# Causal pairs of the third layer alternate with unmasked pairs, under a new table of planner settings

## The chip, the cores and the metric

One core of a Trainium2 chip. The metric is the device time of one execution in microseconds (us), lower is better. The engines are TensorE (PE, matrix products into PSUM), ScalarE (ACT), VectorE (DVE), GpSimd (POOL) and SyncE (SP, which issues the DMAs).

## The reference

Four transformer layers over 2048 tokens of width 512, 32 heads of 16, all in bfloat16. Layers 0 and 2 (kind A; the third layer is layer 2) split the tokens into 4 segments of 512; within a segment attention is causal, and a running memory matrix of the earlier segments is mixed in through a gate. Layers 1 and 3 (kind B) are unmasked attention over all 2048 keys. Cut to what matters:

```python
for s in range(4):                                   # layers 0 and 2
    qs, ks, vs = q[:, :, s], k[:, :, s], v[:, :, s]
    p = softmax(einsum('bhqd,bhkd->bhqk', qs, ks) * scale + mask)
    a_dot = einsum('bhqk,bhkd->bhqd', p, vs)
    a_mem = (phi(qs) @ M) / (phi(qs) @ z + 1e-6)
    outs.append(g * a_mem + (1 - g) * a_dot)
    M, z = M + phi(ks).T @ vs, z + phi(ks).sum()
...
p = softmax(einsum('bhqd,bhkd->bhqk', q, k) * Dh ** -0.5)   # layers 1 and 3
x = x + attention(layernorm(x)) @ wo                        # every layer
```

## The kernel before

The cost is in the exponentials of the scores. The kernel works in tiles of 128 keys by 512 queries for one head. Eight heads share a chunk `c` of 128 rows; a *group* is the four even or four odd heads (`e`) of a chunk for one segment of queries, and the two groups of a chunk make a *pair*. An unmasked group against all keys has 64 tiles; a causal group of 12 has the tiles `k2`, `k13` and `k0` (256, 512 and 512 columns), which leave out the masked blocks.

A *unit* is two or three tiles in adjacent PSUM banks: PE writes the scores (L445), one ACT instruction takes the exponential of up to 1536 columns into `pT` (L1514), POOL clears the masked triangle of causal tiles (L1529), and two or three units later PE multiplies by the values into one accumulator bank. Two sets of three banks alternate between units. Beside this, DVE computes the exponential of some tiles (`dx`): a first step (`dx_first`, L1121) writes scaled scores as integers whose bits are a bfloat16, and two or three shifts (`dx_shift`, L1184) give its further terms; each term has a value product of its own on PE. Such tiles need free DVE time, buffers (`dxw`, and the space of tensors no longer in use), and a free bank. Only unmasked tiles are taken (`dx_find`).

The program has no loop on the chip: a planner in Python writes all instructions out, with its own estimates of when each engine is free. `attention` goes from unit to unit; `select` picks the next pair from two lists, `seqA` (causal) and `seqB` (unmasked), as soon as its inputs are planned; `compose` decides which tiles go to DVE; `background` puts in projections, layer norms, memory updates and output products where credits (`CR_A`, `CR_W`, `CR_LOW`) allow; `keep_busy` adds a product of `zero` with `wB` (a *filler*) where PE would otherwise be thinly used (`FILL`, `FILLS`). `TAKEN` limits how many tiles of a group go to DVE, `REST` and `DQ` when one may be taken, `LOW` and `AHEAD` tell when work is short. The class holds a value of each setting, and the table `PIECES` changes them at times of the planner's own clock for ACT, about every 40 us.

The lines that the change touches in effect are those of `select` (L1392 on):

```python
        if not self.ALT and len(self.sel) > 2 and self.seqA and self.seqA[0][0].L and all(g.kind == "B" and not g.pos for g in tail) and ...:
            ...                                   # an unmasked pair not yet begun is handed back
            self.seqB.insert(0, tail)
        while len(self.qm_free) > 1 and (...):
            pair = None
            spread = self.ALT and self.seqA and self.seqA[0][0].L and self.seqA[0][0].qseg < self.ALTS and (0 < self.run_b < self.ALT or self.run_a >= self.ALTA[self.seqA[0][0].qseg])
            for seq in (self.seqB, self.seqA) if spread else (self.seqA, self.seqB):
                if seq and self.met(self.group_needs(seq[0][0])):
                    pair = seq.pop(0)
                    self.run_a, self.run_b = (self.run_a + 1, 0) if pair[0].kind == "A" else (0, self.run_b + 1)
                    break
```

With `ALT = 0` the causal list always comes first: all pairs of a segment of the third layer whose inputs are there run in a row, ahead of unmasked pairs of the second layer. When both kinds are chosen, the masked queries of a pair (`qm`, L1424) are made on DVE, else on POOL.

Of the kernel before, what the change touches and what calls it, by code (L numbers as in the profile page):

```python
# [257 lines left out]
class Builder:  # L258
    NPU, NDX, FIT, MARGIN, PART, FILL_DVE, EARLY, FILL = 4, 5, 2, 450, 1, 300, 700, 0.5
    FILLS, DVE_FIN, DX_FIN, EVAC_ACT, DX_BANK, DX_LATE, BG_BANK, DVE_LATE = 2, 600, 2000, 0, 500, 3000, 200, 1000  # L260
    DVE_LATE_LOW, CR_A, CR_B, CR_W, CR_LOW, CARRY, CARRY_W, REST = 9000000000.0, 1300, 1500, 1400, 1900, 0, 0, 11
    NEAR, SLACK, ALT3, ALT5, GAP, AHEAD, PE_B, PE_A = 10, 300, 2, 4, 2, 300, 4, 5
# [5 lines left out]
    DX_RES, CHAINS, ALT, ALTS, ALTA = 0, 4, 0, 3, (1, 1, 1, 1)  # L268
# [12 lines left out]
              (420.0, {'DMA_LATE': 300, 'DMA_STEPS': 3, 'DQ': 2500, 'DX_RES': 2, 'DX_T': 330, 'FILLS': 1, 'HOR': 100, 'MARGIN': 700, 'NEAR': 6, 'NEAR_E': 0, 'NEAR_N': 200}),  # L281
              (460.0, {'ALTA': (1, 9, 9, 9), 'DMA_LATE': 300, 'DMA_STEPS': 3, 'DQ': 2500, 'DX_RES': 2, 'DX_T': 330, 'FILLS': 1, 'HOR': 100, 'MARGIN': 700, 'NEAR': 10, 'NEAR_E': 0, 'NEAR_N': 200, 'TAKEN': 1.5}),
              (500.0, {'ALTA': (1, 1, 9, 9), 'CR_W': 1250, 'DMA_LATE': 600, 'DMA_STEPS': 2, 'DQ': 2200, 'DQN': 300, 'DX_RES': 0, 'DX_T': 430, 'FILLS': 2, 'HOR': 400, 'MARGIN': 450, 'NEAR_E': 60, 'NEAR_N': 130, 'TAKEN': 2.7}),
              (540.0, {'ALTA': (1, 1, 1, 1), 'CR_W': 1400, 'DQ': 2500, 'DQN': 600, 'PE_A': 4}),
              (580.0, {'DQ': 2200, 'FILLS': 1, 'FILL_DVE': 450, 'PART': 3, 'PE_A': 5}),
              (620.0, {'FILLS': 1, 'FILL_DVE': 450, 'NEAR_S': 30, 'PART': 3, 'SLACK': 150}),
              (660.0, {'FILLS': 2, 'FILL_DVE': 300, 'NEAR_S': 60, 'PART': 1, 'SLACK': 0}),
              (700.0, {'MARGIN': 700, 'SLACK': 0, 'TAKEN': 2.4}),
              (740.0, {'DQ': 2500, 'DX_LATE': 1500, 'MARGIN': 700, 'SLACK': 0, 'TAKEN': 2.4}),
              (780.0, {'DQ': 2200, 'DX_LATE': 3000, 'MARGIN': 450, 'PVHOLE': 250, 'PVLATE': 600, 'SLACK': 300, 'TAKEN': 2.7}),  # L290
              (820.0, {'BG_BANK': 0, 'PVHOLE': 100, 'PVLATE': 900, 'TAKEN': 3}),
              (860.0, {'AHEAD': 200, 'BG_BANK': 200, 'TAKEN': 2.7}),
# [1593 lines left out]
```

## Time and profile before

| | us |
|---|---|
| median of 3 runs | 1779.52 |
| lowest, highest | 1776.07, 1780.4 |
| the profiled execution | 1777.42 |
| its span | 1775.7 |
| ACT busy | 1733.2 (98%) |
| PE busy | 1586.7 (89%) |
| DVE busy | 1520.6 (86%) |
| POOL busy | 287.4 (16%) |

The span is the stretch from the first to the last instruction. Each line of a profile names the engine, the line of the kernel, the operation, the tiles written and read (out<-in), their shapes, and the count; "idle before" is the time the engine sat idle just before, with what ended it.

### The profile page before, as it was taken

What the parts mean: (1) busy time and instruction counts of PE and PEld (TensorE: products, weight loads), DVE (VectorE), ACT (ScalarE), POOL (GpSimd) and SP (SyncE); (2) the same over time, 40 slices, a digit from 0 to 9 for tenths busy, and PEclk for the clock granted to TensorE, in tenths of its full rate; (3) what the DMA queues carried; (4) which work ended last, traced back from release to release, by engine and by line L of the source; (5) the groups of instructions that cost most, each with busy time, mean ns of one, the idle gap of its engine ahead of it and who ended that gap; (6) DMA issues with size and microseconds to landing.
All of it is one profiled execution on the core that took longest, in us unless ns stands there. A gap on an engine that the chain in (4) does not pass through costs nothing.

```text
span 1775.7 us, 42674 instructions
## 1 busy us (share of the span) xinstructions
PE 1586.7 (89%) x17429; PEld 564.7 (32%) x17429; DVE 1520.6 (86%) x3016; ACT 1733.2 (98%) x1680; POOL 287.4 (16%) x656
## 2 busy tenths in 40 slices
PE   8889899999998999999999989999888888888887
PEld 4445454452223222323222332332222222222222
DVE  6677867499985999798999789767999999999998
ACT  7999999999999999999999999999999999999998
POOL 4622415110005000203000330241100000000000
PEclk9999999999999999999999999999999999999999
DMA  6121111000101000000000010010000000000000
GB/s 173 22 47 32 29 17 26 14 12 4 16 7 16 1 13 13 8 13 19 1 13 13 16 23 13 16 22 13 2 13 1 1 1 13 1 1 7 7 1 13
DMA packets 86180, 30.01 MB, mean 17 GB/s; under 512 B 78816, under 2 KB 85472, under 8 KB 85984
## 3 DMA queue, kind: packets, MB, share of 16 engines
q1 hardware_dynamic: 85984, 27.29, 7.5%
q8 instruction: 136, 2.23, 0.5%
q14 instruction: 60, 0.49, 0.1%
HBM read 6.30 MB, written 2.10 MB: 5 GB/s over the span
## 4 chain that ended last, share of the span: by engine, by line
ACT 50%; PE 22%; issue 16%; DVE 9%; POOL 2%; DMA 1%; SPq 0%; ACTq 0%; DVEq 0%; POOLq 0%
ACT pT L1514 49%; PE ps L445 22%; POOL pT L1529 2%; DVE KB L1121 1%; DVE VB L1121 1%; DVE dxw L1184 1%; ACT amem L697 0%; DVE dxw L1121 0%; DVE QA L1121 0%; DMA xT<-xn 0%; DVE KA L1121 0%; DVE KA L1646 0%; DVE KB L1184 0%; DVE x L911 0%; DVE VB L1184 0%
## 5 line engine op out<-in xcount | busy, mean ns | idle before, releaser
L1514 ACT ACTIVATE pT<-ps 128x1024 bf16<-128x1024 f32 (+4 forms) x1627 | 1700.1, 1193 | 27.9 <-PE ps L445 19.8
L445 PE MATMUL ps<-qm,KB 32*128 32x512 bf16 x3584 | 524.0, 386 | 97.8 <-ACT pT L1514 87.0
L445 PE MATMUL ps<-pT,VB 128*17 128x512 bf16 x2217 | 378.9, 387 | 10.5 <-ACT pT L1514 6.0
L1529 POOL TENSOR_SCALAR_AFFINE_SELECT pT<-pT 128x256 bf16<-128x256 bf16 (+2 forms) x524 | 211.8, 416 | 545.0 <-ACT pT L1514 533.0
L445 PEld LDWEIGHTS ps<-qm,KB 32*128 32x128 bf16 x3584 | 132.3, 91 | 465.7 <-ACT pT L1514 360.5
L1424 POOL TENSOR_SCALAR qm<-QB,par 128x512 bf16<-128x512 bf16 x88 | 68.2, 777 | 856.4 <-PE ps L445 782.8
L445 PEld LDWEIGHTS ps<-pT,VB 128*17 128x17 bf16 x2217 | 87.6, 87 | 244.2 <-issue 198.9
L1121 DVE TENSOR_SCALAR dxw<-ps 128x512 uint16<-128x512 f32 (+1 forms) x209 | 143.6, 698 | 5.3 <-PE ps L445 4.4
L445 PE MATMUL ps<-qm,QA 32*128 32x512 bf16 x512 | 111.4, 391 | 25.4 <-ACT pT L1514 22.7
L1184 DVE TENSOR_SCALAR dxw<-dxw 128x1024 uint16<-128x1024 uint16 (+1 forms) x315 | 125.2, 409 | 3.0 <-PE ps L445 1.3
L1121 DVE TENSOR_SCALAR QA<-ps 128x512 uint16<-128x512 f32 (+1 forms) x174 | 122.2, 715 | 5.4 <-PE ps L445 4.8
L445 PE MATMUL ps<-qm,KA 32*128 32x384 bf16 (+3 forms) x1024 | 103.4, 307 | 24.2 <-ACT pT L1514 20.0
L445 PE MATMUL ps<-VA,pT 128*128 128x51 bf16 (+1 forms) x2560 | 109.0, 189 | 14.0 <-POOL pT L1529 6.4
L1121 DVE TENSOR_SCALAR VA<-ps 128x512 uint16<-128x512 f32 (+1 forms) x159 | 114.0, 730 | 6.3 <-PE ps L445 5.5
L445 PE MATMUL ps<-dxw,VW 128*17 128x512 bf16 x435 | 110.6, 383 | 0.2 <-DVE dxw L1184 0.2
L445 PEld LDWEIGHTS ps<-VA,pT 128*128 128x128 bf16 x2560 | 86.2, 97 | 63.2 <-POOL pT L1529 29.7
L1121 DVE TENSOR_SCALAR KB<-ps 128x512 uint16<-128x512 f32 (+1 forms) x128 | 96.2, 769 | 2.8 <-PE ps L445 1.9
L445 PE MATMUL ps<-xT,wA 128*128 128x512 bf16 (+1 forms) x281 | 78.3, 381 | 1.5 <-DVE xT L658 0.9
L445 PE MATMUL ps<-pT,VA 128*17 128x512 bf16 x393 | 78.6, 387 | 1.2 <-ACT pT L1514 0.9
L1121 DVE TENSOR_SCALAR VB<-ps 128x512 uint16<-128x512 f32 (+1 forms) x99 | 74.7, 769 | 3.2 <-PE ps L445 2.6
L445 PE MATMUL ps<-dxw,VB 128*17 128x512 bf16 x256 | 74.3, 381 | 0.0
L445 PE MATMUL ps<-VB,pT 128*128 128x34 bf16 (+1 forms) x1788 | 69.5, 186 | 1.4 <-ACT pT L1514 1.1
(289 smaller groups left out, 2436.1 us busy)
## 6 DMA issues: line engine op xcount, KB each, us to landing
out_dram<-x SPq DMA_DIRECT2D x8, 256.0 KB, 2.2
x<-in_A_x_dram SPq DMA_DIRECT2D x3, 512.0 KB, 5.1
wB<-in_B_wqkv_dram SPq DMA_DIRECT2D x1, 1536.0 KB, 11.7
xT<-xn SPq DMA_TRANSPOSE x60, 2.4
oT<-ob SPq DMA_TRANSPOSE x36, 2.4
x<-in_A_x_dram SPq DMA_DIRECT2D x4, 128.0 KB, 2.3
wA<-in_A_wq_dram SPq DMA_DIRECT2D x1, 512.0 KB, 4.5
wA<-in_A_wk_dram SPq DMA_DIRECT2D x1, 512.0 KB, 6.1
```

Source lines behind the costliest of these rows:

```text
L445: self.sc.add("pe", lambda e: e.matmul(out, lhsT, rhs, start=start, stop=stop, skip_group_check=True), reads=reads, banks=[(bank, "w", all ...
L1121: self.sc.add("dve", lambda e: e.tensor_scalar(d, o, SCALE * LOG2E * 128, W_C if dxs[0][:3] in self.wt else EXP_C, op0=ALU.mult, op1=ALU.add),
L1184: self.op("dve", lambda e: e.tensor_scalar(o, w, d, None, op0=ALU.add), reads=self.b_dxw[b0][:len(ents)], writes=wr, ns=(295, 425, 560, 69 ...
L1424: self.op(eng, (lambda m, q, col: lambda e: e.tensor_scalar(m, q, col, 0.0, op0=ALU.mult, op1=ALU.add))(m, q, col), reads=[bq, self.b_par] ...
L1514: self.sc.add("act", (lambda dst, src: lambda e: e.activation(dst, src, ACT.Exp, scale=SCALE))(dst, src), writes=self.b_pT[slot * 3 + i:sl ...
L1529: self.op("pool", (lambda blk, pat: lambda e: e.affine_select(blk, blk, pattern=pat, compare_op=ALU.is_ge, fill=0.0, base=0, channel_multi ...
```

## The change

`ALT` goes from 0 to 1 and `ALTS` from 3 to 4. With `ALT = 1` an unmasked pair is no longer handed back, and after `ALTA[segment]` causal pairs of the third layer in a row one unmasked pair goes first, in all four segments (`ALTS = 4`). `ALTA` is 1 unless the table sets it; a 9 means no alternation in that segment. All entries of the table from 420 us on are new. No line of code outside these constants changes. The diff, with part of the table:

```diff
@@ -265,7 +265,7 @@ class Builder
     QREST, CLOSE, FM, NAREA, XDX, NEAR_S, NEAR_E, DX_WAIT = 24, ('proj', 2, 2), 3, 18, 99, 60, 60, 400
-    DX_RES, CHAINS, ALT, ALTS, ALTA = 0, 4, 0, 3, (1, 1, 1, 1)
+    DX_RES, CHAINS, ALT, ALTS, ALTA = 0, 4, 1, 4, (1, 1, 1, 1)
...
@@ -278,40 +278,40 @@ the table PIECES, from 420 us on
-              (420.0, {'DMA_LATE': 300, 'DMA_STEPS': 3, 'DQ': 2500, 'DX_RES': 2, 'DX_T': 330, 'FILLS': 1, 'HOR': 100, 'MARGIN': 700, 'NEAR': 6, 'NEAR_E': 0, 'NEAR_N': 200}),
-              (460.0, {'ALTA': (1, 9, 9, 9), 'DMA_LATE': 300, 'DMA_STEPS': 3, 'DQ': 2500, 'DX_RES': 2, 'DX_T': 330, 'FILLS': 1, 'HOR': 100, 'MARGIN': 700, 'NEAR': 10, 'NEAR_E': 0, 'NEAR_N': 200, 'TAKEN': 1.5}),
-              (500.0, {'ALTA': (1, 1, 9, 9), 'CR_W': 1250, 'DMA_LATE': 600, 'DMA_STEPS': 2, 'DQ': 2200, 'DQN': 300, 'DX_RES': 0, 'DX_T': 430, 'FILLS': 2, 'HOR': 400, 'MARGIN': 450, 'NEAR_E': 60, 'NEAR_N': 130, 'TAKEN': 2.7}),
-              (540.0, {'ALTA': (1, 1, 1, 1), 'CR_W': 1400, 'DQ': 2500, 'DQN': 600, 'PE_A': 4}),
-              (580.0, {'DQ': 2200, 'FILLS': 1, 'FILL_DVE': 450, 'PART': 3, 'PE_A': 5}),
...
-              (1060.0, {'AHEAD': 300, 'CARRY_W': 300, 'DVE_FIN': 600, 'DX_LATE': 3000, 'DX_RES': 0, 'FILL': 0.35, 'FILL_DVE': 300, 'MARGIN': 450, 'PART': 1, 'REST': 11, 'REST_N': 20}),
-              (1140.0, {'CARRY_W': 0, 'DMA_STEPS': 2, 'DXA_REST': 10, 'FILL': 0.5, 'FILLS': 3, 'LOW': 4, 'PVN': 3, 'REST_N': 14}),
-              (1300.0, {'AHEAD': 200, 'BG_BANK': 400, 'DVE_FIN': 1000, 'DX_RES': 1, 'FILLS': 3, 'FILL_DVE': 150, 'LOW': 4, 'MARGIN': 700, 'NEAR_S': 30, 'PVN': 2}),
-              (1460.0, {'AHEAD': 200, 'BG_BANK': 400, 'DVE_FIN': 1000, 'DX_RES': 1, 'EVAC_ACT': -300, 'FILL': 0.45, 'FILLS': 2, 'FILL_DVE': 150, 'LOW': 4, 'MARGIN': 700, 'NEAR_S': 30, 'PVN': 2, 'REST': 14, 'REST_N': 20}),
...
+              (420.0, {'DMA_LATE': 600, 'DMA_STEPS': 2, 'DQ': 2200, 'DXS': 0, 'DX_RES': 0, 'DX_T': 480, 'FILLS': 2, 'HOR': 400, 'MARGIN': 450, 'NEAR_E': 60, 'NEAR_N': 130, 'PVN': 2}),
+              (460.0, {'CR_LOW': 2200, 'DXS': 1, 'DX_T': 430, 'FILL': 0.45, 'PVN': 4}),
+              (500.0, {'ALTA': (2, 9, 9, 9), 'CR_LOW': 1900, 'DXS': 0, 'FILL': 0.5}),
+              (540.0, {'AHEAD': 500, 'ALTA': (2, 9, 9, 9), 'DXS': 0, 'DX_LATE': 1500, 'REST': 8}),
+              (580.0, {'AHEAD': 300, 'ALTA': (9, 9, 9, 9), 'DXS': 1, 'DX_FIN': 1500, 'DX_LATE': 3000, 'FILL': 0.45, 'REST': 11}),
+              (620.0, {'ALTA': (9, 9, 9, 9), 'DVE_LATE': 3000, 'DX_FIN': 1500, 'FILL': 0.45, 'NEAR_S': 0, 'PE_LOW': 5}),
+              (660.0, {'ALTA': (1, 1, 1, 1), 'DVE_LATE': 1000, 'DX_FIN': 2000, 'FILL': 0.5, 'FILL_DVE': 700, 'NEAR_S': 60, 'PE_LOW': 6, 'SLACK': 150}),
+              (700.0, {'CR_W': 1550, 'DX_T': 380, 'FILL_DVE': 700, 'NEAR_N': 100, 'SLACK': 150}),
+              (780.0, {'ALTA': (2, 2, 2, 9), 'CR_A': 1500, 'CR_W': 1550, 'DX_BANK': 300, 'DX_RES': 1, 'DX_T': 380, 'FILL_DVE': 700, 'NEAR_N': 100, 'SLACK': 150}),
+              (820.0, {'ALTA': (2, 2, 2, 9), 'CR_A': 1500, 'CR_W': 1550, 'DXS': 2, 'DX_BANK': 300, 'DX_RES': 1, 'DX_T': 380, 'FILL_DVE': 700, 'MARGIN': 700, 'NEAR_N': 100, 'SLACK': 150}),
+              (860.0, {'ALTA': (1, 1, 1, 1), 'CR_A': 1300, 'CR_W': 1400, 'DXS': 1, 'DX_BANK': 500, 'DX_RES': 0, 'DX_T': 380, 'FILL_DVE': 300, 'MARGIN': 450, 'NEAR_N': 130, 'SLACK': 300}),
...
+              (1020.0, {'ALTA': (9, 9, 9, 9), 'DX_BANK': 500, 'DX_LATE': 5000, 'DX_RES': 0, 'DX_T': 430, 'DX_WAIT': 400, 'REST_N': 20, 'TAKEN_N': 3}),
+              (1060.0, {'ALTA': (1, 1, 1, 1), 'DX_LATE': 3000, 'PART': 4, 'REST': 8, 'REST_N': 14, 'TAKEN': 3}),
+              (1100.0, {'FILL_DVE': 150, 'PART': 1, 'REST': 11, 'TAKEN': 2.7}),
+              (1300.0, {'DQN': 1500, 'DXS': 2, 'DX_T': 480, 'TAKEN': 3}),
+              (1420.0, {'DMA_STEPS': 2, 'DQN': 600, 'DXS': 1, 'DX_T': 430, 'FILLS': 3, 'TAKEN': 2.7}),
+              (1460.0, {'FILL': 0.45, 'FILLS': 2}),
+              (1580.0, {'BG_BANK': 400, 'DQ': 2500, 'DX_T': 480, 'FILL': 0.45, 'FILL_DVE': 700, 'PVHOLE': 250}),
...
```

41 lines of the change are left out of this document (16 added, 25 removed).

## The prediction

> **What bounds the kernel now.** First the page: the shares of the engines, and the chain that ended last.
>
> ```profile
> span 1775.7 us, 42674 instructions
> PE 1586.7 (89%) x17429; PEld 564.7 (32%) x17429; DVE 1520.6 (86%) x3016; ACT 1733.2 (98%) x1680; POOL 287.4 (16%) x656
> ACT 50%; PE 22%; issue 16%; DVE 9%; POOL 2%; DMA 1%; SPq 0%; ACTq 0%; DVEq 0%; POOLq 0%
> ```
>
> ScalarE (ACT) is busy for 1733.2 of 1775.7 us; 42.5 us are left. It holds half of the chain, TensorE (PE) 22%. Next, the table of waits, for what ACT waits for:
>
> ```profile
> ACT pT L1514 <- PE ps L445: 19.8, 45, 2.1
> ```
>
> That is the scores of the next unit, written by PE. So the time is ACT's own work plus the places where PE is late. Where those are, busy time by stretch shows (columns: stretch, PE, weight loads, DVE, ACT, POOL, then the granted TensorE clock):
>
> ```profile
> 0.00:400.00 400.00, 358.79 (x5593) 199.35 (x5594) 283.66 (x676) 377.59 (x370) 134.50 (x317) 0.99 0.19 41
> 400.00:550.00 150.00, 140.08 (x1364) 43.58 (x1362) 133.94 (x273) 149.18 (x150) 15.56 (x36) 1.00 0.06 10
> 550.00:600.00 50.00, 45.80 (x504) 16.02 (x504) 39.98 (x80) 48.36 (x52) 13.89 (x34) 0.97 0.07 10
> 600.00:1050.00 450.00, 420.25 (x4028) 131.71 (x4028) 402.64 (x831) 446.79 (x454) 63.22 (x155) 1.00 0.07 12
> 1050.00:1100.00 50.00, 45.08 (x377) 12.62 (x376) 46.65 (x105) 48.52 (x47) 2.78 (x4) 0.94 0.08 17
> 1100.00:1150.00 50.00, 46.21 (x432) 15.16 (x428) 40.16 (x89) 49.17 (x47) 8.75 (x23) 0.99 0.07 14
> 1150.00:1200.00 50.00, 45.67 (x518) 19.34 (x516) 31.73 (x73) 47.55 (x45) 21.28 (x51) 0.93 0.11 23
> 1200.00:1400.00 200.00, 172.37 (x1548) 46.02 (x1548) 184.16 (x319) 198.70 (x183) 14.38 (x22) 1.00 0.03 6
> 1400.00:1450.00 50.00, 41.55 (x414) 10.43 (x412) 48.68 (x79) 49.21 (x45) 3.01 (x3) 0.97 0.01 1
> 1450.00:1500.00 50.00, 43.58 (x428) 11.82 (x424) 48.38 (x85) 50.00 (x51) 1.38 (x2) 1.00 0.04 12
> 1500.00:1550.00 50.00, 40.52 (x387) 9.88 (x385) 47.40 (x73) 48.60 (x45) 2.32 (x3) 0.93 0.00 1
> 1550.00:1750.00 200.00, 167.87 (x1690) 43.52 (x1690) 194.29 (x311) 200.00 (x186) 6.32 (x7) 1.00 0.01 4
> 1750.00:1776.00 26.00, 18.99 (x178) 5.29 (x177) 18.94 (x36) 19.56 (x18) 0.00 (x0) 1.00 0.06 21
> ```
>
> Of ACT's idle time 22.4 us lie in the first 400 us and 6.4 us in the tail after 1750. Between 400 and 1750, nearly all that the change can reach, 13.9 us are left, 1.0%. Of these 8.6 us lie in the six stretches of 50 us whose granted clock is below 1.00 (1.64, 1.48, 0.83, 2.45, 0.79, 1.40). The other 21 stretches of that length share 5.3 us, 0.25 us each. So better overlap has little to give; a gain must come from less work on ACT.
>
> **What the change does to the instruction lists.** Both programs can be listed without being run. They are the same up to unit 293 of 1549, close to 400 us. Before, the pairs of the third layer stand in five stretches: segment 0 whole, segment 1 as two halves, segments 2 and 3 whole. After, in nine: 2+2, 1+1+2, 1+1+2, and segment 3 still whole. The work is the same set of 4864 score tiles; what differs is how many DVE takes off ACT (1039 before, 1052 after) and how ACT's share is cut into instructions.
>
> **ACT's work.** The groups by form:
>
> ```profile
> L1514 ACT ACTIVATE pT<-ps 128x1536 bf16<-128x1536 f32 x606 | 872.1, 1501 | 16.3 <-PE ps L445 11.4 <-POOL pT L1529 1.8 <-POOL VB L882 0.9
> L1514 ACT ACTIVATE pT<-ps 128x1024 bf16<-128x1024 f32 x862 | 847.6, 1079 | 8.8 <-PE ps L445 6.4 <-POOL pT L1529 1.0 <-ACT pT L1514 0.2
> L1514 ACT ACTIVATE pT<-ps 128x768 bf16<-128x768 f32 x48 | 41.3, 861 | 1.2 <-PE ps L445 0.9
> L1514 ACT ACTIVATE pT<-ps 128x512 bf16<-128x512 f32 x55 | 31.0, 654 | 0.6 <-PE ps L445 0.5
> L1514 ACT ACTIVATE pT<-ps 128x256 bf16<-128x256 f32 x56 | 24.3, 434 | 0.9 <-PE ps L445 0.7
> L478 ACT ACTIVATE QB<-ps 128x512 bf16<-128x512 f32 x4 | 2.4, 603 | 0.0
> ```
>
> These durations overlap, so they aren't the price. The timeline of ACT shows runs without a gap, and the groups of the same windows the mean of one:
>
> ```profile
> 1303.43 10.19 ACT L1514 ACTIVATE pT<-ps 128x1024 bf16<-128x1024 f32 x11 [0.35 <-PE ps L445]
> 334.62 9.51 ACT L1514 ACTIVATE pT<-ps 128x1536 bf16<-128x1536 f32 x7 [0.20 <-PE ps L445]
> L1514 ACT ACTIVATE pT<-ps 128x1024 bf16<-128x1024 f32 x11 | 10.2, 1074 | 0.4 <-PE ps L445 0.4
> L1514 ACT ACTIVATE pT<-ps 128x1536 bf16<-128x1536 f32 x7 | 9.5, 1474 | 0.2 <-PE ps L445 0.2
> ```
>
> Start to start, 1024 columns take (10.19-1.07)/10 = 0.912 us and 1536 take (9.51-1.47)/6 = 1.340 us. A tile of 512 columns more is thus 0.428 us, and an instruction overlaps its neighbour by about 1.079-0.912 = 0.167 us. The lists after against before: 825 against 862 of 1024 columns, 628 against 606 of 1536, 59 against 56 of 256, 47 against 48 of 768, 50 against 55 of 512, and two copies out of PSUM fewer. That is -37 x 0.912 = -33.7; +22 x 1.340 = +29.5; +3 x 0.267 = +0.8; -0.7; -5 x 0.487 = -2.4; -2 x 0.436 = -0.9: **-7.4 us** on the path. By the busy means it would be -10.9 us; I take the cadence, because ACT is nearly always fed.
>
> [...]
>
> Where it lies: from unit 293 to the fourth layer's start ACT has 6 tiles more in 12 units fewer (+6 x 0.428 - 12 x (0.912 - 0.856) = +1.9 us). In the fourth layer's segment 0, with the third layer's last segment, it has 17 fewer (512 to 495: -7.3 us), in the other segments 2 fewer (-0.9). So the alternation itself saves ACT nothing; the gain comes later, by tiles put where DVE has room.
>
> **Does DVE have that room?** Its rows:
>
> ```profile
> L1121 DVE TENSOR_SCALAR dxw<-ps 128x512 uint16<-128x512 f32 x203 | 136.3, 682 | 4.5 <-PE ps L445 3.7
> L1184 DVE TENSOR_SCALAR dxw<-dxw 128x1024 uint16<-128x1024 uint16 x271 | 112.6, 425 | 2.4 <-PE ps L445 1.3
> L1121 DVE TENSOR_SCALAR KB<-ps 128x1024 uint16<-128x1024 f32 x21 | 25.5, 1215 | 0.2 <-PE ps L445 0.2
> L1184 DVE TENSOR_SCALAR QA<-QA 128x2048 uint16<-128x2048 uint16 x48 | 32.7, 682 | 0.2 <-PE ps L445 0.2
> L1424 DVE TENSOR_SCALAR qm<-QA,par 128x512 bf16<-128x512 bf16 x63 | 22.6, 400 | 0.5 <-ACT QA L761 0.3
> ```
>
> The lists of DVE change by -41 first steps of 512 columns and +27 of 1024, +41 shifts of 1024 and -16 of 2048, +8 masked queries (off POOL): -41 x 0.682 + 27 x 1.215 + 41 x 0.425 - 16 x 0.682 + 8 x 0.400 = +14.6 us, with small forms some 16. 18 of the tiles added lie in the fourth layer's segment 0, which begins at the edge near 1040 us (shown below). Between 1050 and 1200 DVE is idle for 3.35 + 9.84 + 18.27 = 31.5 us; 18 tiles at 0.68 for the first step and three shifts of half 0.425 each take 24 us. They fit, and cost nothing as long as PE feeds both; if not, the saved 7.3 us turn into waits (a rival below). After 1200 DVE is at 92% and more (97% after 1550) and the tiles there change by 5 - 4 + 0: no new bound.
>
> **The new edges.** Where a stretch of third-layer pairs gives way to unmasked ones, DVE already takes tiles of the next pair while masked tiles pass ACT, PE turns to another accumulator, and ACT sits idle once. The timeline of ACT at the five edges before, the last the first unmasked unit after segment 3:
>
> ```profile
> 564.70 1.45 ACT L1514 ACTIVATE pT<-ps 128x1536 bf16<-128x1536 f32 x1 [0.87 <-PE ps L445]
> 754.31 2.02 ACT L1514 ACTIVATE pT<-ps 128x256 bf16<-128x256 f32 x3 [0.34 <-PE ps L445]
> 821.60 1.02 ACT L1514 ACTIVATE pT<-ps 128x1024 bf16<-128x1024 f32 x1 [1.03 <-PE ps L445]
> 1038.65 1.02 ACT L1514 ACTIVATE pT<-ps 128x1024 bf16<-128x1024 f32 x1 [0.40 <-POOL pT L1529]
> 1176.09 2.98 ACT L1514 ACTIVATE pT<-ps 128x1536 bf16<-128x1536 f32 x2 [2.13 <-PE ps L445]
> ```
>
> The first four are alike (tiles of the next pair on DVE) and average 0.66 us; the fifth is the wait for the fourth layer's later keys. The change adds four of the alike kind and gives the fifth such tiles too: nine against four, 5 x 0.66 = 3.3 us if each costs as before, 0 if the idle time goes with the number of masked tiles, which is the same. Below nothing isn't excluded: the table is a new one, and all 13.9 us between 400 and 1750 could shrink. I take the middle, +1.6 us, because the 0.87 stands in the stretch whose clock was 0.97, so that the mean holds some of the clock's cost. What else is queued: each masked unit's values wait on PE for POOL's mask, and stand ahead of the next unit's scores; that is within these prices.
>
> **Filler matmuls.** PE gets 29 more of them, 204 against 175.
>
> ```profile
> 820.24 0.59 PE L445 MATMUL ps<-wB,zero 128*128 128x512 bf16 x2
> L445 PE MATMUL ps<-wB,zero x175: 376/379/635, 37.6 to 1750.2; 128*128 128x512 bf16 x175
> ```
>
> Two take 0.59 us, one 0.38: 0.21 us each in a row, 6 us of PE in all. 23 of the 29 come in the fourth layer's segment 1 (30 against 7), where the old schedule has PE at 86% (1200 to 1400). They hide in PE's idle time; without it they would delay the scores of their unit by 0.2 to 0.4 us each, 6 us at most. I count them at nothing.
>
> **Sum.** The profiled execution took 1777.42 us, its span is 1775.7. 1777.4 - 7.4 + 1.6 = 1771.6. The three timed runs have their median at 1779.52, 2.1 above the profiled one; so I forecast a median of **1773.7 us**, 0.33% less. A difference under 0.3% (5.3 us) can't be told from no change here: the three runs of before are 4.3 us apart.
>
> **Rivals.**
> *Each edge costs its full price.* With the lost overlap 0.66 + 0.167 = 0.83 us, 5 x 0.83 = 4.1: 1779.5 - 7.4 + 4.1 = 1776.2, no change. For it: four edges of four before have their idle time. Against it: it is their worst single one each.
> *The clock stays up.* The six stretches with a lowered clock hold 8.6 - 6 x 0.25 = 7.1 us of excess idle time on ACT. If the 29 fillers keep PE at full clock there, this goes too: 1773.7 - 7.1 = 1766.6. For it: the idle time and the lowered clock fall together in all six. Against it: filler stood in the old schedule as well, and the fall may be the result of the wait, not its cause. [...]
> *The edges cost what the worst one cost (slower).* The edge at 1176 us, where PE got its operands late, cost 2.13 us. The four added edges put a short masked stretch of 8 units between unmasked pairs; if PE, coming back, finds its keys, masks or accumulator late each time, nine such edges cost 19.2 us against 4.8 before: 1779.5 - 7.4 + 14.4 = 1786.5. It decides from (4.8 + 7.4 + 5.3)/9 = 1.94 us an edge. For it: one of five did. Against it: that one waited for keys of the last segment, which inner edges don't.
> *The gain is not one.* ACT's 7.3 us fewer in the fourth layer's segment 0 fall where it already idles 4.8 us (1050 to 1200); if PE sets the pace there, they turn into idle time, and the alternation's own 1.9 us stay: 1779.5 - 7.4 + 7.3 + 1.6 = 1781.0, no change. For it: PE's clock is lowest there. Against it: ACT is still busy 97% of that stretch.
>
> **How the numbers follow.** Forecast 0.44, which with its own spread of 3 us falls to 0.30 below 1774.2 and 0.14 above; full price of the edges 0.18; clock 0.18; slower edges 0.13; gain lost 0.07. Faster by over 0.3%: 0.30 + 0.18 = 0.48. Within 0.3%: 0.14 + 0.18 + 0.07 = 0.39. Slower: 0.13. The range runs from the clock's case less a us (1765.5) to just over the lost gain (1782); the slower edges and a little at the low end stay outside. The forecast's own range is 1770.5 to 1777.
>
> **What the profile after would show.** ACT busy near 1722 us, by -37, +22 and the small forms as listed; the same first 400 us, nearly; no long masked stretch but the last. Right about the edges: nine waits of 0.3 to 1 us before L1514 where masked tiles end, some 15 us of idle time on ACT between 400 and 1750. The clock's case: hardly a stretch under 1.00 and under 10 us idle. Wrong: over 27 us idle there (edges of 2 us, or fillers ahead of scores in the fourth layer's segment 1), or exponentials that take longer than 0.912 and 1.340 us start to start, which no row above allows for.

## The result, and the profile after

| | before | after |
|---|---|---|
| median, us (7 runs each) | 1778.78 | 1783.23 |
| lowest, highest | 1776.07, 1780.4 | 1781.76, 1787.0 |
| profiled execution, its span | 1777.42, 1775.7 | 1783.23, 1781.5 |

The changed kernel is slower: ratio 1.0033, 95% interval 1.0022 to 1.0045. The forecast was 1773.7 us, with a range that ended at 1782.0. The page of after, its shares and its chain:

```profile
span 1781.5 us, 42588 instructions
PE 1579.0 (89%) x17291; PEld 571.4 (32%) x17480; DVE 1535.8 (86%) x3037; ACT 1727.5 (97%) x1660; POOL 280.6 (16%) x655
ACT 44%; PE 27%; issue 15%; DVE 10%; POOL 2%; DMA 1%; SPq 0%; ACTq 0%; DVEq 0%; POOLq 0%
```

ACT is busy 5.7 us less, as it was meant to be, and the span is 5.8 us longer: ACT stands idle 11.5 us more (54.0 against 42.5). PE's share of the chain has grown from 22% to 27%. The table of waits and the groups by form of after:

```profile
ACT pT L1514 <- PE ps L445: 31.6, 65, 2.8
L1514 ACT ACTIVATE pT<-ps 128x1536 bf16<-128x1536 f32 x628 | 907.0, 1504 | 23.6 <-PE ps L445 19.2 <-POOL pT L1529 2.2 <-POOL qm L1424 0.3
L1514 ACT ACTIVATE pT<-ps 128x1024 bf16<-128x1024 f32 x825 | 820.8, 1085 | 12.2 <-PE ps L445 9.6 <-POOL pT L1529 0.6
```

Waits for scores rose from 19.8 us in 45 places to 31.6 in 65. The instructions themselves take as long as before (1504 and 1085 ns against 1501 and 1079). The granted clock of TensorE (a share of full speed) is not the reason: its mean over the span is 0.993, before 0.989. It rather hides a part of the loss. The 58 executions of before that were timed beside the experiments run from 1783.27 us at a mean clock of 0.985 to 1770.17 at 0.997, some 1.1 us less for each 0.001 more. At 0.993 they took 1773.2 to 1775.4 us, and the three of after at 0.993 took 1782.8 to 1784.7. At the same clock the change thus costs some 9 us (estimated from these executions).

Where the waits are is read from busy time by stage. A stage begins with the first exponential of its first unit: from unit 293 to the first masked unit of the third layer (S1); from there to the start of the fourth layer, the part in which the pairs alternate (S2); the first wave of the fourth layer's segment 0 (W1); the third layer's last segment (M3); the rest of segment 0 (W2); and the three other segments. Windows of after, with columns as in the prediction's table:

```profile
396.70:532.50 135.80, 123.81 (x1152) 36.41 (x1164) 127.63 (x251) 133.48 (x130) 2.22 (x3) 0.97 0.05 10
532.50:1051.90 519.40, 464.11 (x4661) 155.23 (x4719) 447.28 (x936) 508.87 (x505) 82.76 (x218) 1.00 0.07 12
1051.90:1143.80 91.90, 84.43 (x717) 24.65 (x725) 85.37 (x182) 90.49 (x86) 5.08 (x9) 1.00 0.07 14
1143.80:1184.50 40.70, 35.05 (x511) 17.85 (x516) 28.16 (x66) 37.52 (x42) 25.86 (x66) 0.98 0.14 24
1184.50:1285.40 100.90, 87.38 (x722) 25.30 (x728) 90.81 (x184) 95.17 (x83) 15.11 (x24) 0.99 0.04 8
1285.40:1451.30 165.90, 147.94 (x1375) 39.22 (x1380) 161.47 (x252) 164.96 (x153) 6.11 (x8) 1.00 0.01 4
1451.30:1609.90 158.60, 140.60 (x1344) 37.58 (x1346) 154.83 (x248) 158.43 (x149) 5.85 (x8) 1.00 0.02 5
1609.90:1781.50 171.60, 149.95 (x1380) 37.83 (x1383) 160.05 (x259) 164.70 (x155) 3.95 (x5) 1.00 0.02 7
```

And S1, S2 and W2 of before, cut in the same way:

```profile
396.30:525.90 129.60, 123.19 (x1145) 36.12 (x1146) 125.09 (x246) 128.78 (x128) 2.47 (x3) 1.00 0.06 8
525.90:1040.50 514.60, 478.43 (x4719) 154.18 (x4718) 445.95 (x925) 509.62 (x522) 88.83 (x220) 1.00 0.06 12
1176.10:1277.20 101.10, 91.67 (x719) 25.95 (x718) 80.26 (x164) 100.03 (x87) 11.84 (x19) 0.98 0.06 12
```

For a balance, each ACT instruction is given the time from its start to the next one's when nothing is late: 1.330 us for 1536 columns and 0.903 for 1024 (the lowest 2% of the trace), and so on for the small forms. What a start comes later than that is called starvation. So each stage is ACT's work plus starvation (us, before to after):

| | S1 | S2 | W1 | M3 | W2 | seg. 1 | seg. 2 | seg. 3 | all |
|---|---|---|---|---|---|---|---|---|---|
| length | 129.6 to 135.8 | 514.6 to 519.4 | 95.5 to 91.9 | 40.1 to 40.7 | 101.1 to 100.9 | 163.5 to 165.9 | 165.7 to 158.6 | 169.3 to 171.6 | +5.8 |
| ACT's work | 126.2 to 130.2 | 499.1 to 497.3 | 90.5 to 88.3 | 37.1 to 36.6 | 98.2 to 92.0 | 160.2 to 162.4 | 160.3 to 155.8 | 159.8 to 161.2 | -7.6 |
| starvation | 3.4 to 5.5 | 15.5 to 22.0 | 5.0 to 3.6 | 3.0 to 4.1 | 3.0 to 9.0 | 3.3 to 3.4 | 5.4 to 2.8 | 6.2 to 7.2 | +13.3 |

(The columns "all" include the first 400 us: work equal, starvation 0.5 more, length 0.4 more.) Three things stand out. S1 loses 6.2 us before the first masked pair of the third layer has come. S2 starves 6.5 us more. In W2 ACT has 6.2 us less to do, and the stage is as long as before; its DVE column goes from 80.26 to 90.81.

What such waits look like: the timeline of after around the longest, in M3 (other lines in between left out):

```profile
1177.58 0.43 DVE L899 TENSOR_TENSOR oT<-oT,phq 128x512 bf16<-128x512 bf16 x1 [1.06 <-DMA phq<-amem]
1177.92 0.68 DVE L822 TENSOR_TENSOR amem<-ps,rg 128x512 bf16<-128x512 f32 x1
1179.99 2.67 SPq L487 DMA_TRANSPOSE phq<-amem  x2
1180.39 0.43 DVE L899 TENSOR_TENSOR oT<-oT,phq 128x512 bf16<-128x512 bf16 x1 [1.78 <-DMA phq<-amem]
1180.73 0.68 DVE L822 TENSOR_TENSOR amem<-ps,rg 128x512 bf16<-128x512 f32 x1
1181.33 0.60 DVE L1424 TENSOR_SCALAR qm<-QB,par 128x512 bf16<-128x512 bf16 x2
1181.73 0.09 PEld L445 LDWEIGHTS ps<-qm,QA 32*128 32x128 bf16 x1 [2.12 <-DVE qm L1424]
1182.26 2.37 ACT L1514 ACTIVATE pT<-ps 128x1024 bf16<-128x1024 f32 x2 [2.80 <-PE ps L445]
```

Read upward from the last line. ACT waits 2.80 us for scores; PE waits 2.12 for masked queries (`qm`, L1424), which DVE makes; DVE stands 1.78 us in L899, which adds the memory's part to the output, for the transfer that transposes this part (`phq<-amem`); the read-out L822 and the queries are queued behind it. The queries don't need that part; the read-out writes a buffer that such a transfer reads, which matters below. Before, the last queries of this place were made on POOL, and L899 never waited for that transfer: its row holds one other wait alone. In after, DVE waits another 2.04 us in this instruction at 978.58, and ACT 1.46 us at 980.80. The row of before:

```profile
L899 DVE TENSOR_TENSOR oT<-oT,phq 128x512 bf16<-128x512 bf16 x24 | 10.2, 437 | 3.8 <-DMA oT<-ob 3.8
```

In W2 PE waits for DVE as well, here for the same addition (behind another transfer) and for L1606, which adds an accumulator bank to a sum and so sets the bank free:

```profile
1193.01 0.42 DVE L899 TENSOR_TENSOR oT<-oT,phq 128x512 bf16<-128x512 bf16 x1 [1.22 <-DMA oT<-ob]
1193.49 0.39 PE L445 MATMUL ps<-woA,oT 128*128 128x512 bf16 x1 [0.82 <-DVE oT L899]
1194.63 1.45 ACT L1514 ACTIVATE pT<-ps 128x1536 bf16<-128x1536 f32 x1 [1.47 <-PE ps L445]
1204.25 0.60 PE L445 MATMUL ps<-pT,VA 128*17 128x512 bf16 x6 [1.21 <-DVE KB L1606]
1205.02 1.45 ACT L1514 ACTIVATE pT<-ps 128x1536 bf16<-128x1536 f32 x1 [1.13 <-PE ps L445]
```

### The profile page after: what moved, and what is told of

The parts are those of the page before. It is cut to its first block, busy times and chain, and to the rows that moved or that the text cites. A ratio compares the mean times of both kernels' runs of the same rounds, so it can differ in the third digit from the quotient of the medians.

```text
span 1781.5 us, 42588 instructions
## 1 busy us (share of the span) xinstructions
PE 1579.0 (89%) x17291; PEld 571.4 (32%) x17480; DVE 1535.8 (86%) x3037; ACT 1727.5 (97%) x1660; POOL 280.6 (16%) x655
## 4 chain that ended last, share of the span: by engine, by line
ACT 44%; PE 27%; issue 15%; DVE 10%; POOL 2%; DMA 1%; SPq 0%; ACTq 0%; DVEq 0%; POOLq 0%
ACT pT L1514 43%; PE ps L445 27%; POOL pT L1529 2%; DVE dxw L1184 1%; DVE dxw L1121 1%; DMA xT<-xn 1%; DVE QA L1121 1%; ACT amem L697 0%; DMA phq<-amem 0%; DVE VA L1121 0%; DVE VB L480 0%; DVE x L911 0%; DVE KB L1121 0%; DVE KB L480 0%; DVE ob L1628 0%
## 5 line engine op out<-in xcount | busy, mean ns | idle before, releaser
L1514 ACT ACTIVATE pT<-ps 128x1024 bf16<-128x1024 f32 (+4 forms) x1609 | 1695.2, 1204 | 39.0 <-PE ps L445 31.6
L1529 POOL TENSOR_SCALAR_AFFINE_SELECT pT<-pT 128x384 bf16<-128x384 bf16 (+2 forms) x531 | 212.9, 412 | 721.9 <-ACT pT L1514 709.0
L1121 DVE TENSOR_SCALAR dxw<-ps 128x512 uint16<-128x512 f32 (+1 forms) x254 | 176.9, 711 | 6.3 <-PE ps L445 5.0
L1424 POOL TENSOR_SCALAR qm<-QB,par 128x512 bf16<-128x512 bf16 x80 | 60.9, 763 | 690.7 <-PE ps L445 621.2
L1184 DVE TENSOR_SCALAR dxw<-dxw 128x1024 uint16<-128x1024 uint16 (+1 forms) x356 | 140.9, 412 | 6.2 <-PE ps L445 3.7
L445 PE MATMUL ps<-dxw,VW 128*17 128x512 bf16 x554 | 127.2, 385 | 0.6 <-DVE dxw L1184 0.6
L445 PE MATMUL ps<-qm,KA 32*128 32x256 bf16 (+3 forms) x1024 | 105.5, 307 | 24.5 <-ACT pT L1514 19.1
L1121 DVE TENSOR_SCALAR VA<-ps 128x512 uint16<-128x512 f32 (+1 forms) x140 | 102.5, 748 | 9.3 <-PE ps L445 8.8
L445 PEld LDWEIGHTS ps<-VA,pT 128*128 128x128 bf16 x2560 | 86.2, 97 | 66.3 <-POOL pT L1529 31.5
L1121 DVE TENSOR_SCALAR QA<-ps 128x512 uint16<-128x512 f32 (+1 forms) x135 | 100.2, 757 | 4.2 <-PE ps L445 3.5
L445 PE MATMUL ps<-dxw,VB 128*17 128x512 bf16 x303 | 84.0, 381 | 0.4 <-DVE dxw L1184 0.4
L1121 DVE TENSOR_SCALAR KB<-ps 128x512 uint16<-128x512 f32 (+1 forms) x103 | 77.4, 766 | 2.8 <-PE ps L445 2.5
L445 PE MATMUL ps<-xT,wA 128*128 128x512 bf16 (+1 forms) x232 | 63.6, 381 | 5.1 <-issue 3.0
```

The lines of the kernel that those rows point to most:

```text
L445: self.sc.add("pe", lambda e: e.matmul(out, lhsT, rhs, start=start, stop=stop, skip_group_check=True), reads=reads, banks=[(bank, "w", all ...
L1121: self.sc.add("dve", lambda e: e.tensor_scalar(d, o, SCALE * LOG2E * 128, W_C if dxs[0][:3] in self.wt else EXP_C, op0=ALU.mult, op1=ALU.add),
L1184: self.op("dve", lambda e: e.tensor_scalar(o, w, d, None, op0=ALU.add), reads=self.b_dxw[b0][:len(ents)], writes=wr, ns=(295, 425, 560, 69 ...
L1424: self.op(eng, (lambda m, q, col: lambda e: e.tensor_scalar(m, q, col, 0.0, op0=ALU.mult, op1=ALU.add))(m, q, col), reads=[bq, self.b_par] ...
L1514: self.sc.add("act", (lambda dst, src: lambda e: e.activation(dst, src, ACT.Exp, scale=SCALE))(dst, src), writes=self.b_pT[slot * 3 + i:sl ...
L1529: self.op("pool", (lambda blk, pat: lambda e: e.affine_select(blk, blk, pattern=pat, compare_op=ALU.is_ge, fill=0.0, base=0, channel_multi ...
```

## Experiments

The kernel names begin with a where after is edited, with b where before is. The plan (which instruction stands where) stays as it is, except in the three kernels of the second part.

### Which engine sets the pace: exponentials at half width

ACT's instructions, DVE's, or both work on half of their columns from unit 293 on. The value products keep their shape; the numbers are meaningless, the plan, order and waits stay. The ACT edit, and DVE's in its core:

```diff
+            if n >= 293:
+                src = src[:, :, 0:w // 2]
-            dst = self.pT[:, slot, i:j + 1, 0:w]
+            dst = self.pT[:, slot, i:j + 1, 0:w // 2 if n >= 293 else w]
...
+        cut = 256 if self.units >= 293 else 512
-        o = bcast(self.ps[:, banks[0].col0:banks[0].col0 + 1], [[step, k], [1, 512]])
+        o = bcast(self.ps[:, banks[0].col0:banks[0].col0 + 1], [[step, k], [1, cut]])
```

> The changed kernel with the same plan, but from unit 293 on each exponential covers half the columns (the other half of the scores keeps older values), so that ACT's work is about halved there. What is left of each stage is what PE, DVE and the transfers need with this order. If ACT sets the pace everywhere, all stages shorten by a quarter or more. If PE and DVE set the pace in the fourth layer's second wave over segment 0 (100.9 us, of which ACT worked 92), that stage stays above 95 us while the others shorten; the 6.2 us of exponentials saved there were then never to be had.

> The kernel before with the same plan, but from unit 293 on each exponential covers half the columns, as in the changed kernel's run of that kind. If the changed kernel's second wave is paced by PE and DVE, this one's (101.1 us, of which ACT worked 98) comes down to 92-96 us, under the changed kernel's. If ACT sets the pace in both, both come down alike, to under 85.

> The changed kernel with the same plan; from unit 293 on the first steps and shifts of the tiles on DVE cover half the columns (their value products read that half twice), so DVE's exponentials cost about half. Half the exponentials on ACT took only 37 us off this kernel, so ACT alone does not set the pace. If DVE does in the fourth layer, its second wave (100.9 us) comes down to about its ACT work, 92 to 94, and the last three segments (496 us) to about 480; the whole run then ends no later than the kernel before with the same edit, since ACT has 7 us less to do. If PE and the order of its work set the pace, the run shortens by less than 15 us and stays 4 us or more above the other.

> The kernel before with the same edit: DVE's exponentials half as wide from unit 293 on. If DVE set the changed kernel's pace, this one gains less in the second wave (101.1 us, of which ACT worked 98), 2 to 3 us, and ends level with the changed kernel's run or later. If PE sets the pace, it ends 4 us or more earlier than that.

> The changed kernel with both edits, exponentials half as wide on ACT and on DVE from unit 293 on: what PE, POOL, the transfers and the waits between engines need with this order. If the three engines are balanced, 1560 to 1650 us; if PE sets the pace throughout, within 20 us of the run with ACT alone halved, 1725 or more.

> The kernel before with both edits. If the alternation costs PE nothing, it is level with the changed kernel's run within 3 us; if the nine masked stretches with their fillers and edges cost PE more than the five, it is 4 us or more shorter, and the difference lies between 400 and 1050 us.

Measured, one execution each, with the stages cut as above (us):

| | time | S1 | S2 | W2 |
|---|---|---|---|---|
| before, after | 1777.42, 1783.23 | 129.6, 135.8 | 514.6, 519.4 | 101.1, 100.9 |
| ACT half (b_half, a_half) | 1737.53, 1745.86 | 128.6, 130.9 | 494.1, 497.9 | 95.7, 101.1 |
| DVE half (b_dvehalf, a_dvehalf) | 1769.34, 1777.57 | 129.0, 134.0 | 512.3, 518.3 | 100.7, 98.5 |
| both (b_pe, a_pe) | 1567.6, 1607.79 | 116.8, 118.5 | 462.3, 463.1 | 87.8, 91.3 |

The page of a_half, and its window over W2:

```profile
PE 1587.4 (91%) x17291; PEld 581.3 (33%) x17480; DVE 1527.8 (88%) x3037; ACT 1216.0 (70%) x1660; POOL 282.2 (16%) x655
1156.60:1257.70 101.10, 88.20 (x725) 24.97 (x734) 91.17 (x184) 56.86 (x83) 16.06 (x24) 0.95 0.06 8
```

ACT loses 511 us of work (1727.5 to 1216.0) and the kernel gains 37 us, 2%. So ACT, busy for 97% of the span, does not set the pace alone: DVE and what waits for it stand 2% behind. Halving both is worth 10% (after) and 12% (before); there PE, busy for 93 to 94% of the span, comes next.

These are single executions, and with one plan S2 and W2 differ by some 1 and 2 us from one execution to the next (W2 took 100.9 us in after, 102.3 in a_nophq, 102.9 in a_cut, below). In W2 of after, ACT's work falls to 56.86 us and the stage stays at 101.1, with the clock at 0.95 against 0.99: there ACT does not set the pace. Nor does DVE's exponential work alone. Halving it takes 2.4 us off, where 92 to 94 us were expected if it did; the two waits of ACT shown above fall from 1.47 and 1.13 us to 0.22 and 0.19, which is nearly all of this, and 98.5 us are still 6.5 above ACT's work. Halving both leaves 91.3. What sets those 6.5 us is not shown. In before W2 falls by 5.4 us with ACT halved and by 0.4 with DVE halved: there it was ACT. S1 of after is ACT's (135.8, or 134.4 in executions without a lowered clock there, to 130.9). S2 is longer in after by 3.8 us with ACT halved, by 6.0 with DVE halved, and by 0.8 with both: as far as single executions tell, what costs there is neither engine's sum of work, nor PE's, but waits between them.

With DVE halved after ends 8.2 us later than before, which had been named as the sign of PE and the order of its work. With both halved it ends 40 us later, but not between 400 and 1050 us as was expected: 28 us of it lie in the fourth layer's last three segments, where PE is then busy for 95 to 98% in both kernels. The matmuls there are nearly the same, but for 29 fillers against 8; what stretches them so in after is not shown. With whole exponentials after's three segments together are 2.4 us the shorter.

### The settings or the alternation

`b_alt1_plain` has before's table without its entries for `ALTA`, and `ALT = 1`: it alternates after every causal pair, which is more often than after does. `a_alt0` has after's table and before's rule for the order; `a_s1` has before's settings (`ALTA` apart) at 420, 460 and 500 us in after. All three are planned anew.

```diff
 b_alt1_plain:
-    DX_RES, CHAINS, ALT, ALTS, ALTA = 0, 4, 0, 3, (1, 1, 1, 1)
+    DX_RES, CHAINS, ALT, ALTS, ALTA = 0, 4, 1, 4, (1, 1, 1, 1)
 a_alt0:
-    DX_RES, CHAINS, ALT, ALTS, ALTA = 0, 4, 1, 4, (1, 1, 1, 1)
+    DX_RES, CHAINS, ALT, ALTS, ALTA = 0, 4, 0, 3, (1, 1, 1, 1)
 a_s1:
-              (420.0, {'DMA_LATE': 600, 'DMA_STEPS': 2, 'DQ': 2200, 'DXS': 0, 'DX_RES': 0, 'DX_T': 480, 'FILLS': 2, ...
+              (420.0, {'DMA_LATE': 300, 'DMA_STEPS': 3, 'DQ': 2500, 'DX_RES': 2, 'DX_T': 330, 'FILLS': 1, ...
...
```

> The alternation alone: the kernel before with ALT = 1 and ALTS = 4, its table kept but without its entries for ALTA, so that ALTA is 1 throughout. It has 1024 tiles on DVE instead of 1039 and 94 small exponentials instead of 55. If the order of the pairs decides, it is near the changed kernel, 1780-1790. If the table is fitted to one order and worthless with another, it is slower than both by 1.5% or more, over 1805.

> The table alone: the changed kernel with ALT = 0 and ALTS = 3, its table kept. 1024 tiles on DVE instead of 1052. If the new table makes the loss and the alternation is harmless, it is near the changed kernel or slower by a little, 1780-1795. If table and order only work together, it is slower than both by 1.5% or more, over 1805.

> After with the settings at 420, 460 and 500 us put back to those of before, except the run lengths of the alternation; everything later is planned anew from there, so only the stretch up to the first masked unit of the third layer is to be read, not the whole time (planned later: 1780 to 1830). Theory 'the new settings, not the alternation, cost the 6.2 us of that stretch': it takes 129 to 131 us as before, with 106 tiles on DVE. Rival 'the alternation costs it there as well' (it changes what is ready, or the clock was down at 439): 133 to 136 us.

Measured: b_alt1_plain 1826.04 us, ratio 1.0267 (1.0238 to 1.0295); a_alt0 1822.0, 1.0244 (1.0217 to 1.0271). Alternation with the old table costs 2.7%, the new table without alternation 2.4%: each table fits the order that it was made for. How much of after's own loss is the order's can't be read from these two, as they were planned anew and put fewer tiles on DVE. In a_s1 (1819.7 in all) S1 takes 129.6 us, with 126.2 of ACT's work and 3.4 of starvation, as in before. So the 6.2 us of S1 are the price of the settings from 420 us on, which put 102 tiles on DVE there instead of 106. Of them 4.0 are ACT's work. The rest is starvation, about 1.4 us of it with a lowered clock in the profiled execution (0.76 over the 14 us from 436): in a_lag, a_cut and a_fill16, which have the same plan for S1 and no such dip there, S1 took 134.4.

### The fillers

In `a_fill16` and `b_fill16` the fillers among the third layer's pairs are 16 columns wide instead of 512. In `a_cut` only those of six units (433, 485, 674, 682, 883, 1000), where a masked pair changes from even to odd heads, ten matmuls in all.

```diff
 a_fill16, b_fill16:
-            self.mm(self.ps[:, bank.col0:bank.col0 + 512], self.zero[:, :], self.wB[:, 0, 0:512], not own, not own,
+            w = 16 if any(h.kind == "A" and h.L for h in [g] * (g is not None) + self.sel[:1]) else 512
+            self.mm(self.ps[:, bank.col0:bank.col0 + w], self.zero[:, :], self.wB[:, 0, 0:w], not own, not own,
 a_cut:
+            w = 16 if self.unit_no in (433, 485, 674, 682, 883, 1000) else 512
```

> The changed kernel with the same plan, but each filler product that stands in a masked stretch of the third layer streams 16 columns instead of 512 (it adds zeros either way). If the loss sits at the edges and the fillers ahead of the scores make it (two of 0.21 us at nine edges), ACT's waits of 0.87 and 1.04 us near 550 and 611 us shrink to about 0.5 and the time falls by 2 to 4 us, to 1779-1781. If the late memory read-out of the third layer makes the loss, or the table, the time stays within 1.5 us of 1783.2. If PE's clock falls for want of work, the time rises by 2 us or more.

> Control: the kernel before with the same plan and fillers of 16 columns in the masked stretches of the third layer. It has four edges of the alike kind instead of nine. If fillers at edges cost 0.4 us each, it gains 1 to 2 us (1777); if they cost nothing, no change; if the clock falls, slower.

> After, with the plan unchanged; only the fillers in six units (433, 485, 674, 682, 883, 1000) at which a masked third-layer pair changes from even to odd heads are 16 columns wide instead of 512, ten matmuls in all. Nothing is left out. Theory 'edges': PE reaches the next scores 0.2 to 0.4 us sooner at each, ACT's waits at 550 and 611 fall from about 0.9 and 1.0 to 0.5 and 0.6, about 2 us in all: 1781, ratio 1.0015. Rival 'the work is balanced' (time won at one wait is lost at the next, since ACT, DVE and PE are all nearly full): under 0.5 us, 1783, ratio 1.003.

Measured: a_fill16 1801.49 us, ratio 1.0139 (1.0118 to 1.0159); b_fill16 1784.82, 1.0044 (1.0028 to 1.006). The window of a_fill16 over S2, nearly, and its waits:

```profile
530.00:1063.00 533.00, 476.52 (x4666) 163.10 (x4712) 448.64 (x938) 511.80 (x505) 82.46 (x218) 0.93 0.06 12
ACT pT L1515 <- PE ps L446: 41.4, 71, 2.9
```

The granted clock falls from 1.00 to 0.93 in this stage and the stage grows by 13 us, though PE was given less to stream. Over the whole span its mean is 0.965 to 0.972 in the executions of a_fill16, against 0.990 to 0.994 in after; in b_fill16 it is 0.971 to 0.979, against 0.985 to 0.997 in before. So in both kernels the fillers are worth more than they cost: the clock stays up with them, and in the alternating order more hangs on them (some 19 us, by the ratios 1.0139 and 1.0033) than in the old one (some 8 us, by 1.0044). What the clock goes by, no run shows.

a_cut: 1783.86 us, ratio 1.0038 (1.0027 to 1.005): no gain in the median. Three of the six edges, in after and in a_cut, by the timeline of ACT; after first:

```profile
549.91 6.88 ACT L1514 ACTIVATE pT<-ps 128x1536 bf16<-128x1536 f32 x6 [0.87 <-PE ps L445]
610.92 5.54 ACT L1514 ACTIVATE pT<-ps 128x1536 bf16<-128x1536 f32 x5 [1.04 <-PE ps L445]
829.37 5.61 ACT L1514 ACTIVATE pT<-ps 128x1024 bf16<-128x1024 f32 x6 [0.69 <-PE ps L445]
```

```profile
545.10 11.83 ACT L1515 ACTIVATE pT<-ps 128x1536 bf16<-128x1536 f32 x10 [0.49 <-PE ps L446]
605.73 10.49 ACT L1515 ACTIVATE pT<-ps 128x1536 bf16<-128x1536 f32 x9 [0.66 <-PE ps L446]
823.71 10.98 ACT L1515 ACTIVATE pT<-ps 128x1024 bf16<-128x1024 f32 x10 [0.31 <-PE ps L446]
```

Each wait falls by 0.38 us, as the theory of the edges said; a fourth, at 1049 us, does too. But the time is the same. The rival's forecast of the time came true, its mechanism (what is won at one wait is lost at a later one) did not. Set beside after start by start, a_cut keeps these 1.5 us until the clock dips: it loses 1.4 us near 985 us (clock 0.75 over 12 us, against 0.86 in after) and 2.5 near 1190 (0.57 over 16 us, against 0.89). W2, where nothing was changed, has its 102.9 instead of 100.9 us from this, at a clock of 0.94 against 0.99. At equal clocks the executions of a_cut are 1.7 us below those of after (an estimate from a straight line through the time and the mean clock of each, good to about 0.5). Whether the missing work on PE lowered the clock in a_cut, 0.992 against 0.993 in the mean, stays open.

### The transfers of the memory's part

`a_nophq`: in the third layer, L899 neither adds nor awaits the memory's part. `a_both`: this and a_fill16's edit. `a_lag` and `b_lag`: besides, the read-out L822 doesn't await the transfer before it (which stays, but reads another tensor).

```diff
 a_nophq:
-                    self.op("dve", (lambda o, m: lambda e: e.tensor_tensor(o, o, m, ALU.add))(o, m),
+                    w = self.op("dve", (lambda o, m: lambda e: e.tensor_tensor(o, o, m, ALU.add))(o, o if L else m),
...
+                    if L:
+                        w.deps = [d for d in w.deps if d is not self.b_phq[c].last_write]
 a_lag, b_lag, besides:
+                if L:
+                    w.deps = [d for d in w.deps if not d.is_dma]
-                self.dma_tr(..., self.amem[:, c % 2, :, :].rearrange("p t q -> p (t q)"),
+                self.dma_tr(..., self.woA[:, c, :] if L else self.amem[:, c % 2, :, :].rearrange("p t q -> p (t q)"),
```

> The changed kernel with the same plan, but in the third layer the addition of the memory part to the attention part (L899) adds the attention part to itself and so waits no more for the transposed memory part; the memory part is left out of that layer's output. If the third layer's lag makes the loss, DVE's 4.9 us of waiting for that transpose goes, and with it ACT's waits of 1.46 us near 981 and 2.80 us near 1182: 4 us, to about 1779. If edges or table make it, the time stays within 1.5 us of 1783.2.

> Both edits together, short fillers in masked stretches and no wait for the memory part (left out of the third layer). If both are causes of their own: 6 to 8 us, 1775-1777, below the kernel before. If the two waits hide each other or go over into others: no more than the better of the two alone.

> After, with the plan unchanged; in the third layer only, the DVE's addition of the memory part (L899) neither uses nor waits for that part, and the DVE's read-out (L822) no longer waits for the transposing transfer of the read-out before it; the transfer itself stays but reads another tensor. Left out: the memory part of that layer. Theory 'transfer lag' (DVE, standing in its queue for those transfers, holds back keys, shifts and operands that PE needs, and ACT starves): ACT's waits of 1.46 us at 981 and 2.80 us at 1182 go, 3 to 4 us in all: about 1779 to 1780, ratio 1.0005 to 1.001. Rival 'edges' (ACT starves at the change from even to odd heads, with PE's order the cause): 1782 to 1783, ratio 1.002 to 1.0025, and other waits take their place.

> The same edit on the kernel before, as a control: it has the same 24 additions and read-outs. Theory 'transfer lag': there the transfers came early, so nothing changes, 1778 to 1779. Rival: it gains as much as after does (1775 to 1776), and the transfers don't tell the two kernels apart.

Measured: a_nophq 1782.79 us, ratio 1.0035 (1.0023 to 1.0047); a_both 1798.99, 1.0125 (1.0108 to 1.0143), the slowdown of a_fill16 again; a_lag 1779.11, 1.0017 (1.0003 to 1.0031); b_lag 1779.07, 1.0008 (0.9995 to 1.002). The groups of the read-out and the addition by form, in after, in a_nophq and in a_lag (where line 899 is 902):

```profile
L822 DVE TENSOR_TENSOR amem<-ps,rg 128x512 bf16<-128x512 f32 x24 | 16.4, 685 | 3.3 <-PE ps L445 2.0 <-DMA phq<-amem 1.3
L899 DVE TENSOR_TENSOR oT<-oT,phq 128x512 bf16<-128x512 bf16 x24 | 10.6, 446 | 6.1 <-DMA phq<-amem 4.9 <-DMA oT<-ob 1.2
```

```profile
L822 DVE TENSOR_TENSOR amem<-ps,rg 128x512 bf16<-128x512 f32 x24 | 16.5, 686 | 7.1 <-DMA phq<-amem 5.2 <-PE ps L445 1.8
```

```profile
L822 DVE TENSOR_TENSOR amem<-ps,rg 128x512 bf16<-128x512 f32 x24 | 16.5, 686 | 4.9 <-PE ps L445 4.7
L902 DVE TENSOR_TENSOR oT<-oT 128x512 bf16<-128x512 bf16 x12 | 5.2, 432 | 2.1 <-DMA oT<-ob 2.1
```

Taking one wait away (a_nophq) moved it to the next instruction that hangs on the same transfer, 5.2 us in place of 1.3, and the time stayed. With both gone (a_lag), ACT's wait near 981 is gone and that of 2.80 us is 0.83:

```profile
1180.01 0.75 DVE L1429 TENSOR_SCALAR qm<-QB,par 128x512 bf16<-128x512 bf16 x2
1180.94 2.37 ACT L1519 ACTIVATE pT<-ps 128x1024 bf16<-128x1024 f32 x2 [0.83 <-PE ps L445]
```

M3 takes 38.7 us instead of 40.7, and the last part of S2 (from 921 us) 128.6 instead of 131.0; 1.5 and 2.0 us of this are the two waits at 981 and 1182. Earlier in the same execution 1.5 us are lost at 823 us, where ACT waits 2.07 us instead of 0.53 while the clock is at 0.72 (818 to 824). By its median a_lag is level with b_lag (1779.11, 1779.07), but only because its clock was higher, 0.994 against 0.990 in the mean. At equal clocks, by the same straight lines, a_lag is 2.6 us below after (good to about 0.5) and b_lag level with before. So these transfers cost after some 3 us and before nothing that can be seen. By the ratios alone the intervals of after and a_lag overlap; the 3 us rest on the clocks and the traces.

## Why the prediction was wrong, point by point

The forecast was a sum: ACT's work, -7.4 us, and waits, +1.6. ACT's work came as forecast. The waits are the term that failed: starvation rose by 13.3 us, of which 6.5 lie in S2, 6.0 in W2 and 2.1 in S1 (some other stages had less).

- **ACT's work, -7.4 us: right.** The balance gives -7.6, in the places named (+2.2 to the fourth layer's start against +1.9 forecast, -8.9 in its segment 0 with the third layer's last segment against -7.3, -0.9 in the others).
- **The step that failed first is the premise: "better overlap has little to give; a gain must come from less work on ACT".** ACT's 1.0% of idle time between 400 and 1750 us was read as if nothing but ACT could set the pace. a_half shows that the next bound stands 2% behind ACT: less work on ACT turns into gain only where DVE and the waits behind it leave room.
- **"They fit, and cost nothing": wrong in W2.** 31.5 us of idle DVE time between 1050 and 1200 was counted for tiles of the fourth layer's segment 0. But 9 of the tiles are begun in W2 (43 to 52, by the columns of their first steps), most of which lies after 1200, where the prediction had DVE at 92%. There DVE went from 80.26 to 90.81 us, and 6.2 us less work on ACT made the stage 0.2 shorter. This is what the rival *The gain is not one* forecast, at a chance of 0.07 and 7.3 us of loss; it cost 6.0. The rival named PE. ACT's two longest waits there stand behind PE's for DVE, and 2.4 us go when DVE's exponentials are halved; the rest of the 6.0 stays open.
- **"+1.9 us" from unit 293 to the fourth layer: right as a sum, and it hid two parts.** S1 alone has 4.0 us more work for ACT and is 6.2 longer, S2 has 1.8 less work. The change was read as alternation; the settings from 420 us were not costed where they act alone.
- **The edges, +1.6 us: too small.** S2 starves 6.5 us more, M3 1.1. The ordinary edge was sized well: 0.87, 1.04, 0.69, 0.70 us, against 0.66 forecast. What the sum had no term for are waits of 1.46 and 2.80 us where DVE, in its order, stands on a transfer; in before L899 had no wait for it. The prediction counted the 8 masked queries moved to DVE by their duration (8 x 0.400), and did not name what they queue behind. The rival of the worst price named late operands, as it came; but it came at two places and not at nine, and its 1786.5 us overshot.
- **The fillers "at nothing": right about the time, not the reason.** They do delay scores, by 0.38 us at a change of heads (a_cut), 1.5 us in all; that gain is lost in dips of the clock, and with all of them narrowed the clock falls to 0.93.
- **The clock's rival: half its mechanism.** The clock did stay up (0.97 over the worst stage, S1, and 0.98 to 1.00 elsewhere), which by the 1.1 us for each 0.001 is worth 2 to 4 us; and ACT was starved more all the same. So the 7.1 us that this rival hoped for were in part had, and lost elsewhere.
- **What the profile after was to show.** ACT's idle time between 400 and 1750 us was forecast at some 15; it is 24.84 (the window below), and 27 had been named as the sign of a wrong forecast. ACT's busy time came to 1727.5 and not 1722, as the two large forms took 3 and 6 ns longer each.

```profile
400.00:1750.00 1350.00, 1206.29 (x11557) 365.72 (x11673) 1229.14 (x2324) 1325.16 (x1269) 146.26 (x338) 0.99 0.05 10
```

What stays open: of the starvation in S2 some 1.5 us hang on the transfers and 1.5 on the fillers at four changes of heads; of the 6.0 us more in W2 some 2.4 are DVE's. The rest stands in many short waits, most of them in the stages where the order changes more often; no run took them away, and they can't be put on one cause. None of the runs points to a version that beats before.

## What to carry to other kernels

An engine busy for 97% need not be the bound (here 511 us less work on ACT was worth 37): halve its work without touching the order, and then its neighbour's, and see what each is worth before counting tiles moved between them as a gain. Compare executions at the same granted clock before calling a small change nothing (in before, 0.001 of it went with some 1.1 us). Count room on the receiving engine in the same stage as the tiles, not in a stretch beside it. When an operation moves to another engine's queue, its price can be what stands ahead of it there (here an addition that waited 1.78 us for a transfer), not its own duration (0.60 us for two masked queries).

## What the runs showed of the hardware

Narrowing all the fillers of a stage that lasts 519 us took its granted clock from 1.00 to 0.93 (0.965 to 0.972 over the whole span, against 0.990 to 0.994) and cost the kernel some 19 us (a_fill16), though PE then had less to stream. The clock's dips didn't stay at one place: with the same plan, S1 had one between 436 and 450 us in after (0.76) and none in a_lag (1.00 from 432 to 452), which had one at 818 to 824 (0.72; 1.00 in after). And the time of one plan went with its mean clock: 58 executions of before fall from 1783.27 us at 0.985 to 1770.17 at 0.997.
